# A linear attention, token mixing and gated MLP chain: the list order of all its steps replaced by a written-out order

## The chip, the cores and the metric

The kernel runs on one core of a Trainium2 chip. The core has five engines with an instruction queue each: TensorE (PE in the profile, with its weight loads as PEld), VectorE (DVE), ScalarE (ACT), GpSimd (POOL) and SyncE (SP). Each works off its queue in order and waits at semaphores for the others. DMAs are issued here from SP's and POOL's queues. The metric is the device time of one execution in microseconds; less is better. What is given of a kernel is the median of its runs.

## The reference

```python
def _attn_ref(q, k, v, alpha):              # 4 batches, 8 heads, 768 positions, 48 wide
    for t in range(S):
        state = alpha[:, :, t, :, None] * state + einsum('bhd,bhe->bhde', k[:, :, t], v[:, :, t])
        y[:, :, t] = einsum('bhd,bhde->bhe', q[:, :, t], state)
...
def _moe_ref(x, w_theta, w_tok_r, w_tok_i, w_ch):       # x is 4 x 768 x 384
    theta = x @ w_theta
    y = einsum('ts,bsd->btd', w_tok_r, x * cos(theta)) + einsum('ts,bsd->btd', w_tok_i, x * sin(theta))
    u = x + y
    return u + maximum(u @ w_ch, 0.0)
...
def _moe2_ref(x, w_in, w_spatial, b_spatial, w_out):
    h = maximum(x @ w_in, 0.0)                          # 1024 wide
    u, v = h[..., :512], h[..., 512:]
    v_n = (v - mean(v)) / sqrt(var(v) + 1e-06)
    v_s = einsum('ts,bsd->btd', w_spatial, v_n) + b_spatial[None, :, None]
    return (u * v_s) @ w_out
```

The three run one after the other, the output of each being the x of the next.

## The kernel before

The attention is cut into 24 units: 4 batches with 6 blocks of 128 positions each. A unit holds two chunks of 64 positions for all heads. Large products are made of three passes each: a float32 operand is split into a high part (a cast by ScalarE) and a low part (a subtraction by VectorE), and high by high, high by low and low by high are added up in PSUM.

**A unit's steps in the first stage.** SP loads alpha (`load_al`, tile `al`, two buffers), q and k (`load_qk`) and v (`load_v`). VectorE makes the running products of alpha with two scans and a reciprocal (`att_scan`, L515 to L519, tiles `al` and `heads`) and scales q and k with them (`att_qk`, L527). TensorE makes the scores (`att_a`, L541) and the transposed k (`att_k`, L565); VectorE masks the scores (`att_mask`, L549, tiles `ax` and `am`), one half of which a DMA moves to other partitions (`move_a`, `ay`). State update and output are small products on quarters of the array (`att_u` L582, `att_y` L624; from unit 6 on one step `att_uy` makes the output of a unit and the update of the next), and VectorE takes the state on in short steps (`att_s` L592 writes `ss`, `att_t` L605 writes `tmp`). The last reader of a unit's `al` is its second `att_s`, and with that the load of the unit two later may go. The output x is transposed (`tr_p` L652), split (`tr_h` on ScalarE, `tr_l` L674 on VectorE, tile `xh`) and multiplied by w_theta in two parts (`th_p`, L684 for the high part of x, L687 for the low part). Then theta's fraction is taken (`th_k` on ScalarE, `th_r` L701 on VectorE, tile `r`), cosine and sine are made on ScalarE, multiplied by x (`z_m` L720) and split (`z_h` L724, `z_l` L728, tile `zs`). Token mixing (`tokmix`, L751) multiplies these parts by the token weights, in three column blocks and a real and an imaginary part, and collects a batch's six units in five PSUM banks (tiles `acc`). One bank is set to zero beforehand (`acc_zero`, L760). When a batch is through, VectorE adds x (`evac`, L765), and the channel mixing follows (`ch_h`, `ch_l`, `ch_p` L793, `ch_e` L803).

**The weights.** They are handed in as 64-bit floats. POOL's queue loads 16 pieces (`raw`, two buffers), ScalarE and VectorE make float32 of them (`top` L412, `join` L418) and split them (`high` L430, `low` L438).

**The second stage.** Per batch: v products (`v_p` L930), their norm (`v_r`, `v_b`, `v_w` on POOL, `v_n`) and split, gate products (`g_u` L1003 with the relu `g_r` L1034), spatial mixing (`g_s` L1042 in batch 0; in batches 1 to 3 seven smaller products `g_p` L1071 in place of eight, whose left and right sides are mixed by VectorE), the gating (`g_b`, `g_c`, `g_m` L1108, split by `g_h` and `g_l`) and the output (`o_p` L1129, `o_e`, `o_d`).

**What sets the order.** The code doesn't issue at once: each step is entered in a table with its engine, its cost, the steps that it comes after and the tiles that it holds. `latest` gives every step a due time, counted back from its followers; to it come offsets by the kind of step (the table `OFF`, further ones for the first and last batch, for units and for weight pieces). `order` then goes through a model of the engines and takes, on each free engine, the ready step that is due first. The result is one list, and each engine's queue is that list's steps for it. The last lines are

```python
    with tc.manual_schedule():
        for key in order(latest(steps, due)):
            runs[key](*key[1:])
```

Of the kernel before, what the change touches and what calls it, by code (L numbers as in the profile page):

```python
# [42 lines left out]
T0 = 512  # L43
# [6 lines left out]
OFF = {  # L50
# [6 lines left out]
    "ce": -972.0, "cd": 3157.87, "raw": -151.03, "bits": -1303.6, "sgn": 1953.06, "mag": -330.42, "mul": 468.42,  # L57
    "high": -305.28, "low": 395.16, "v": 17.67, "vr": -218.91, "vb": -247.26, "vw": 2596.17, "vm": 1232.85,
    "vh": -1569.89, "vl": -130.09, "g_u": 11.48, "g_r": -360.31, "g_s": -2682.77, "g_m": -600.69, "g_h": -2547.65,
    "g_l": 1286.47, "o_p": 19.23, "o_e": 2160.27, "x2h": -2423.22, "x2l": 194.68, "x2": 255.08,  # L60
}
SLACK = 1.5
# [8 lines left out]
OFF0 = {  # L71
# [6 lines left out]
}  # L78
OFF3 = {
# [6 lines left out]
}  # L86
UNIT = {
    "0": -1233.88, "1": -299.19, "2": -157.26, "3": -128.17, "4": -124.98, "5": -85.26, "6": -419.5, "7": -274.72,
    "8": -235.21,
}  # L90
PIECE = {
    "0": -1201.98, "1": -1780.19, "2": -1381.94, "3": -878.12, "4": -78.08, "5": 154.16, "6": 764.79, "7": -371.9,
    "8": 64.23, "9": 826.07, "10": 983.66, "11": 1836.51, "12": 3937.87, "13": -2365.1, "14": 839.22, "15": 324.21,
}
# [14 lines left out]
PE_WINDOW = 4096 / 1200  # L109
PE_BUSY = {"att_a": 0.85, "att_u": 0.75, "att_y": 0.75, "att_uy": 0.75}  # L110
QUARTERS = ("att_a", "att_u", "att_y", "att_uy")
TO_QUARTERS = 0.09
TO_WHOLE = 0.12
TOGETHER = 10.0
FIRST = {"pe": 0.8, "dve": 1.6, "act": 2.2, "pool": 1.5, "dma": 0.74, "none": 0.0, "queue": 1.5}
ISSUE = {"dma": 0.44, "queue": 0.57}
AHEAD = {"dma": 0.9, "queue": 1.1}


def order(steps):  # L120

    keys = list(steps)
    at = {k: (round(steps[k][0], 3), n) for n, k in enumerate(keys)}
    follow = {k: [] for k in keys}  # L130
    left = {}
    users = {}
    for k, (_, _, _, _, after, tiles, _) in steps.items():
        left[k] = len(after)
        for p in after:
            follow[p].append(k)
        for x in tiles:
            users[x] = users.get(x, 0) + 1
    held_by = {}
    placed = set()  # L140
    ready = {e: [] for e in ("pe", "dve", "act", "pool", "dma", "none", "queue")}
    free = dict(FIRST)
    quarters = {k: k[0] in QUARTERS for k in keys}
    tiled = False
    port = 0.0
    lines = {"dma": [], "queue": []}
    clock, turn = 0.0, 0
    when = {}
    heap = []
    n = 0  # L150

    def push(t, what, k):
        nonlocal n
        heapq.heappush(heap, (t, n, what, k))
        n += 1

    def rates():
        on = [q for q in lines.values() if q]
        whole = sum(steps[q[0][0]][6] for q in on)
        return [(q, steps[q[0][0]][6] / whole) for q in on]  # L160

    def advance(now):
        nonlocal clock
        for q, r in rates():
            q[0][1] -= (now - clock) * r
        clock = now

    def plan(now):
        nonlocal turn
        turn += 1  # L170
        to = min((now + max(q[0][1], 0.0) / r for q, r in rates()), default=None)
        if to is not None:
            push(to, "moved", turn)

    def finish(k, t):
        push(t, "done", k)
        for f in follow[k]:
            left[f] -= 1
            when[f] = max(when.get(f, 0.0), t)
            if not left[f]:  # L180
                push(when[f], "ready", f)

    for e, t in free.items():
        push(t, "tick", None)
    for k in keys:
        if not left[k]:
            push(0.0, "ready", k)
    out = []
    cold, win, busy = True, 0, {}
    while heap:  # L190
        now = heap[0][0]
        while heap and heap[0][0] <= now + 1e-9:
            _, _, what, k = heapq.heappop(heap)
            if what == "ready":
                heapq.heappush(ready[steps[k][1]], (at[k], k))
            elif what == "done":
                for x in steps[k][5]:
                    users[x] -= 1
                    if not users[x]:
                        held_by[x[0]] -= 1  # L200
            elif what == "sent":
                advance(now)
                lines[steps[k][1]].append([k, steps[k][6]])
                plan(now)
            elif what == "moved" and k == turn:
                advance(now)
                for q in lines.values():
                    if q and q[0][1] < 1e-7:
                        x, _ = q.pop(0)
                        finish(x, now + steps[x][3])  # L210
                plan(now)
        moved = True
        while moved:
            moved = False
            for e, q in ready.items():
                if free[e] > now + 1e-9:
                    continue
                held = []
                while q:
                    if e == "pe" and TOGETHER:  # L220
                        best = min(q, key=lambda x: (x[0][0] - TOGETHER * (quarters[x[1]] == tiled), x[0][1]))
                        q.remove(best)
                        heapq.heapify(q)
                        k = best[1]
                    else:
                        _, k = heapq.heappop(q)
                    _, _, cost, lag, _, tiles, shared = steps[k]
                    fresh = [x for x in tiles if x not in placed]
                    want = {}
                    for x in fresh:  # L230
                        want[x[0]] = want.get(x[0], held_by.get(x[0], 0)) + 1
                    if any(want[x[0]] > x[1] for x in fresh):
                        held.append((at[k], k))
                        continue
                    for x in fresh:
                        held_by[x[0]] = held_by.get(x[0], 0) + 1
                        placed.add(x)
                    out.append(k)
                    moved = True
                    if e == "pe":  # L240
# [21 lines left out]
                    if e != "none":  # L262
                        free[e] = t
                        push(t, "tick", None)
# [1286 lines left out]
```

## Time and profile before

| | us |
|---|---|
| median of 3 runs (594.84 to 598.99) | 595.09 |
| span of the profiled execution, first to last instruction | 592.2 |
| TensorE busy | 561.6 |
| VectorE busy | 440.4 |
| ScalarE busy | 255.5 |
| GpSimd busy | 26.0 |

The profile is of one execution. The time of a run is taken around the whole execution, so it lies a little above a span; 2.9 us lie between this span and the median. Busy times are unions over the span, and a matmul's end is modelled, so a row of TensorE can hold a short delay. In the rows, "PE" is TensorE, "DVE" VectorE, "ACT" ScalarE, and SPq an issue from SyncE's queue; L-numbers are lines of the kernel before.

### The profile page before, as it was taken

What the parts mean: (1) busy time and instruction counts of PE and PEld (TensorE: products, weight loads), DVE (VectorE), ACT (ScalarE), POOL (GpSimd) and SP (SyncE); (2) the same over time, 40 slices, a digit from 0 to 9 for tenths busy, and PEclk for the clock granted to TensorE, in tenths of its full rate; (3) what the DMA queues carried; (4) which work ended last, traced back from release to release, by engine and by line L of the source; (5) the groups of instructions that cost most, each with busy time, mean ns of one, the idle gap of its engine ahead of it and who ended that gap; (6) DMA issues with size and microseconds to landing.
All of it is one profiled execution on the core that took longest, in us unless ns stands there. A gap on an engine that the chain in (4) does not pass through costs nothing.

```text
span 592.2 us, 13513 instructions
## 1 busy us (share of the span) xinstructions
PE 561.6 (95%) x5749; PEld 511.1 (86%) x5749; DVE 440.4 (74%) x770; ACT 255.5 (43%) x475; POOL 26.0 (4%) x45
## 2 busy tenths in 40 slices
PE   1579999999999999999999999999999999999997
PEld 1467878888888898888998899999999899998997
DVE  5999999989787875889355798958636586658650
ACT  2566656435344523544444444434324441435222
POOL 1101100000000000000000001000000010001000
PEclk9999999999999999999999999999999999999999
DMA  7866757435424225333016564001002100210002
GB/s 278 300 219 225 245 185 261 137 99 178 140 93 144 81 69 172 119 99 94 10 52 217 190 226 145 0 1 54 27 2 81 66 14 0 81 68 13 1 1 80
DMA packets 29500, 66.15 MB, mean 112 GB/s; under 512 B 3072, under 2 KB 14336, under 8 KB 29184
## 3 DMA queue, kind: packets, MB, share of 16 engines
q1 hardware_dynamic: 27264, 53.49, 26.8%
q0 software_dynamic: 2176, 11.80, 5.7%
q8 instruction: 45, 0.74, 0.5%
q14 instruction: 15, 0.12, 0.1%
HBM read 52.69 MB, written 9.44 MB: 105 GB/s over the span
## 4 chain that ended last, share of the span: by engine, by line
PE 65%; DVE 16%; DMA 8%; ACT 5%; issue 4%; POOL 1%; SPq 0%; DVEq 0%; POOLq 0%; ACTq 0%
PE acc L751 18%; PE acc L1071 11%; PE pu L1003 7%; PE psc L793 6%; PE po L1129 5%; PE psv L930 5%; PE sp L1042 3%; PE th L684 2%; DMA al<-in_al 2%; PE psuy L624 2%; DVE al L515 2%; DVE qk L527 2%; DMA raw<-in_w_ti 2%; DMA qk<-in_qk 1%; DVE vns L968 1%
## 5 line engine op out<-in xcount | busy, mean ns | idle before, releaser
L751 PE MATMUL acc<-w,zs 128*128 128x512 f32 (+1 forms) x864 | 171.2, 343 | 0.2 <-DVE acc L760 0.2
L751 PEld LDWEIGHTS acc<-w,zs 128*128 128x128 f32 x864 | 133.7, 188 | 17.2 <-DVE acc L760 0.5
L1003 PE MATMUL pu<-xs,w 128*128 128x384 f32 x288 | 53.1, 337 | 1.0 <-ACT ur L1034 0.6
L930 PE MATMUL psv<-w,xs 128*128 128x512 f32 x216 | 53.1, 394 | 0.0
L1129 PE MATMUL po<-w,gs 128*128 128x384 f32 x288 | 52.4, 337 | 0.0
L1003 PEld LDWEIGHTS pu<-xs,w 128*128 128x128 f32 x288 | 50.1, 188 | 2.4 <-ACT v L941 1.0
L1129 PEld LDWEIGHTS po<-w,gs 128*128 128x128 f32 x288 | 50.7, 188 | 0.7
L930 PEld LDWEIGHTS psv<-w,xs 128*128 128x128 f32 x216 | 40.3, 187 | 8.4
L793 PE MATMUL psc<-us,wch 128*128 128x384 f32 (+1 forms) x243 | 41.2, 320 | 0.3 <-DVE xT L803 0.3
L793 PEld LDWEIGHTS psc<-us,wch 128*128 128x128 f32 x243 | 38.0, 189 | 1.3 <-DVE xT L803 0.6
L1115 ACT CAST gs<-t 128x384 fp32r<-128x384 f32 x32 | 16.4, 512 | 50.8 <-DVE t L1108 50.8
L515 DVE TENSOR_TENSOR_SCAN al<-al,heads 112x536 f32<-112x536 f32 x24 | 30.5, 1269 | 7.5 <-DMA al<-in_al 7.5
L953 POOL TENSOR_TENSOR rs<-rs,mhalf 128x1 f32<-128x1 f32 x24 | 15.9, 664 | 441.8 <-DVE rs L950 441.8
L684 PE MATMUL th<-wth,xh 128*128 128x384 f32 x144 | 31.2, 352 | 3.4 <-ACT kt L569 1.0
L724 ACT CAST zs<-z 128x768 fp32r<-128x768 f32 x24 | 20.0, 833 | 27.0 <-PE acc L751 18.8
L728 DVE TENSOR_TENSOR zs<-z,zs 128x768 fp32r<-128x768 f32 x24 | 22.9, 954 | 11.8 <-ACT zs L724 11.5
L519 DVE TENSOR_TENSOR_SCAN al<-al,heads 112x536 f32<-112x536 f32 x24 | 30.6, 1275 | 0.8
L412 ACT ACTIVATE zeros<-raw 128x768 f16<-128x768 bf16 (+1 forms) x22 | 22.8, 1035 | 19.5 <-DMA raw<-in_w_ti 8.3
L684 PEld LDWEIGHTS th<-wth,xh 128*128 128x128 f32 x144 | 25.2, 194 | 6.1 <-ACT xT L661 3.0
L1071 PE MATMUL acc<-wt,vns 128*128 128x384 f32 x162 | 30.4, 338 | 0.0
L1071 PE MATMUL acc<-w,mx 128*128 128x384 f32 x162 | 30.4, 337 | 0.0
L527 DVE TENSOR_TENSOR qk<-qk,al 112x1024 f32<-112x1024 f32 x24 | 29.2, 1219 | 0.1
(122 smaller groups left out, 969.6 us busy)
## 6 DMA issues: line engine op xcount, KB each, us to landing
qk<-in_qk SPq DMA_DIRECT2D x24, 512.0 KB, 4.7
vd<-in_v SPq DMA_DIRECT2D x24, 288.0 KB, 3.9
al<-in_al SPq DMA_DIRECT2D x24, 268.0 KB, 3.7
raw<-in_w_ti POOLq DMA_DIRECT2D x6, 768.0 KB, 5.6
raw<-in_w_tr POOLq DMA_DIRECT2D x6, 768.0 KB, 5.0
out<-o SPq DMA_DIRECT2D x24, 192.0 KB, 1.8
x2d<-xT SPq DMA_DIRECT2D x6, 576.0 KB, 3.3
ay<-ax SPq DMA_DIRECT2D x48, 64.0 KB, 2.3
```

The lines of the kernel that those rows point to most:

```text
L412: nc.scalar.activation(out, c["top"].rearrange("p (c k) -> p c k", k=4)[:, :, 0], AF.Identity, scale=0.5)
L515: nc.vector.tensor_tensor_scan(out=back[:, ::-1], data0=line[:, ::-1], data1=one[:, ::-1], initial=1.0, op0=ALU.mult, op1=ALU.add)
L519: nc.vector.tensor_tensor_scan(out=line, data0=line, data1=one, initial=0.0, op0=ALU.mult, op1=ALU.add)
L527: nc.vector.tensor_tensor(out=x, in0=x, in1=st[u]["ar"], op=ALU.mult)
L684: nc.tensor.matmul(th, xh[:, 0, k], wth[:, pr, k], start=(k == 0 and pr == 0), stop=False)
L728: nc.vector.tensor_tensor(out=zs[:, 1], in0=st[u]["z"], in1=zs[:, 0].bitcast(F32), op=ALU.subtract)
L751: nc.tensor.matmul(acc[b, n][:, c0:c1], zs[:, pl, ri, m * 128:(m + 1) * 128], w[:, pr, t0:t1], start=first and n != 1, stop=last, skip_gro ...
L793: nc.tensor.matmul(ps, wch[:, pl, k, m * 128:(m + 1) * 128], us[:, pr, k], start=(n == 0), stop=(n == 3 * KD - 1),)
L930: nc.tensor.matmul(ps, xs2[:, pl, k, o:o + 128], win[pr, "v"][:, k], start=(n == 0), stop=(n == 3 * KD - 1),)
L1003: nc.tensor.matmul(pu, win[f // 2][:, pl, k * 256 + f % 2 * 128:k * 256 + f % 2 * 128 + 128], xq[b, h][:, pr, k], start=(n == 0), stop=(n ...
L1071: nc.tensor.matmul(g, left(b, n, j, pl, c), right(n, j, pr), start=(n in (1, 5, 6) and i == 0), stop=(i == 3 * NJ - 1), skip_group_check=n ...
L1129: nc.tensor.matmul(po, gs[b][:, pl, f, s * 128:(s + 1) * 128], wo[f // 2][:, pr, f % 2 * DM:(f % 2 + 1) * DM], start=(n == 0), stop=(n == ...
```

## The change

The model, its cost figures and all tables of offsets go. In their place stands `ORDER`, a list of 1709 numbers: the place of each step in the table in which the code enters them. The steps are issued in just that order. What a step issues is unchanged, and so are all tiles and their numbers of buffers. In two entries (`t_h` and `t_l`) a tile is added to those that the step holds; with the model gone, nothing reads that any more.

```diff
-import heapq
...
-OFF = {
-    "al": 696.51, "qk": 555.29, "vt": 1126.11, "sc": -158.32, "kh": -256.6, "q": 2901.57, "A": -999.99, "m": -63.76,
...
-def order(steps):
...
-def latest(steps, due):
...
+ORDER = [int(n) for n in """
+129 130 66 166 131 6 0 167 132 133 67 68 169 69 11 7 168 138 205 134 139 70 140 8 136 1 9 141 170 142 175 12 178 135 165 137 171 176 10 204 13 177 173
...
-            return step(OFF[name] + more.get(name, 0.0) + UNIT.get(str(u), 0.0), eng, cost, fn, u, *args, after=after, tiles=tiles, by=by)
+            return step(0.0, eng, cost, fn, u, *args, after=after, tiles=tiles, by=by)
...
     with tc.manual_schedule():
-        for key in order(latest(steps, due)):
+        keys = list(steps)
+        for key in (keys[n] for n in ORDER):
             runs[key](*key[1:])
```

Of TensorE's 452 steps some 190 keep their place among each other (a longest common sequence), of VectorE's 614 some 310, of ScalarE's 449 some 240, of SP's 152 some 100. The 16 loads on POOL's queue stand as before. No step moves by more than 44 places on its engine. Lines are those of each kernel: the new one is 174 lines shorter above the steps.

The first place is VectorE after the low part of a w_theta piece, where unit 2 is scaled. In the rows, `qk` is the scaling of q and k, `al` with `heads` the scans, `xh` the low part of x, `wf` the joined and `w` the split weight, `ss` a state step, `r` theta's fraction, `ax` and `am` the two masks. Before:

```order
L527 TENSOR_TENSOR qk<-qk,al 112x1024
L592 TENSOR_TENSOR ss<-tmp,al 112x192
L515 SCALAR_TENSOR_TENSOR al<-al,heads 112x536
L518 RECIPROCAL al<-al 112x8
L519 SCALAR_TENSOR_TENSOR al<-al,heads 112x536
L674 TENSOR_TENSOR xh<-pst,xh 128x384
L418 SCALAR_TENSOR_TENSOR wf<-raw,zeros 128x768
L549 TENSOR_TENSOR ax<-acc_383,cst_sb 128x256
L527 TENSOR_TENSOR qk<-qk,al 112x1024
L549 TENSOR_TENSOR am<-acc_384,cst_sb 128x256
L438 SCALAR_TENSOR_TENSOR w<-wf,w 128x768
L674 TENSOR_TENSOR xh<-pst,xh 128x384
```

The same place in the new order:

```order
L353 TENSOR_TENSOR qk<-qk,al 112x1024
L500 TENSOR_TENSOR xh<-pst,xh 128x384
L245 SCALAR_TENSOR_TENSOR wf<-raw,zeros 128x768
L341 SCALAR_TENSOR_TENSOR al<-al,heads 112x536
L344 RECIPROCAL al<-al 112x8
L345 SCALAR_TENSOR_TENSOR al<-al,heads 112x536
L265 SCALAR_TENSOR_TENSOR w<-wf,w 128x768
L418 TENSOR_TENSOR ss<-tmp,al 112x192
L245 SCALAR_TENSOR_TENSOR wf<-raw,zeros 128x768
L527 SCALAR_TENSOR_TENSOR r<-kk,th 128x384
L353 TENSOR_TENSOR qk<-qk,al 112x1024
```

The split of unit 0's x and a weight's join went ahead of unit 3's scan; a split weight, a second join and unit 0's theta went ahead of the scaling of unit 3, and its split of unit 1's x is further down than these rows.

The second place is TensorE when it comes to unit 3: `psk` is the transposed k, `th` the theta products of unit 1, `psa` the scores, `psy` the attention output of unit 2, `acc` with `zs` token mixing. Before:

```order
L565 MATMUL psk<-cst_sb,qk 128x112 x4
L684 MATMUL th<-wth,xh 128x384 x6
L541 MATMUL psa<-qk 64x64 x16
L687 MATMUL th<-wth,xh 128x384 x3
L624 MATMUL psy<-ss,qk 64x48 x4
L624 MATMUL psy<-vd,ay 64x48 x4
```

The same place in the new order:

```order
L391 MATMUL psk<-cst_sb,qk 128x112 x4
L510 MATMUL th<-wth,xh 128x384 x6
L513 MATMUL th<-wth,xh 128x384 x3
L367 MATMUL psa<-qk 64x64 x16
L577 MATMUL acc_513<-w,zs 128x512
L577 MATMUL acc_514<-w,zs 128x256
```

The second theta part went ahead of the scores, and token mixing of unit 0 went ahead of the attention output of unit 2.

The third place is VectorE between the last reading of unit 4's alpha (`ss`, which frees the buffer for unit 6) and the scan of unit 6. `tmp` and `ss` are state steps, `z` and `zs` the product with x and its split. Before:

```order
L592 TENSOR_TENSOR ss<-tmp,al 112x192
L549 TENSOR_TENSOR ax<-psa,cst_sb 128x256
L605 TENSOR_TENSOR tmp<-psu,ss 112x192
L549 TENSOR_TENSOR am<-psa,cst_sb 128x256
L592 TENSOR_TENSOR ss<-tmp,al 112x192
L720 TENSOR_TENSOR z<-z,x 128x768
L418 SCALAR_TENSOR_TENSOR wf<-raw,zeros 128x768
L605 TENSOR_TENSOR tmp<-psu,ss 112x192
L728 TENSOR_TENSOR zs<-z,zs 128x768
L592 TENSOR_TENSOR ss<-tmp,al 112x192
L515 SCALAR_TENSOR_TENSOR al<-al,heads 112x536
```

The same stretch in the new order:

```order
L418 TENSOR_TENSOR ss<-tmp,al 112x192
L245 SCALAR_TENSOR_TENSOR wf<-raw,zeros 128x768
L431 TENSOR_TENSOR tmp<-psu,ss 112x192
L527 SCALAR_TENSOR_TENSOR r<-kk,th 128x384
L554 TENSOR_TENSOR zs<-z,zs 128x768
L265 SCALAR_TENSOR_TENSOR w<-wf,w 128x768
L375 TENSOR_TENSOR ax<-psa,cst_sb 128x256
L418 TENSOR_TENSOR ss<-tmp,al 112x192
L431 TENSOR_TENSOR tmp<-psu,ss 112x192
L245 SCALAR_TENSOR_TENSOR wf<-raw,zeros 128x768
L418 TENSOR_TENSOR ss<-tmp,al 112x192
L341 SCALAR_TENSOR_TENSOR al<-al,heads 112x536
```

Two joins, a split weight and `r` stand in between now, and a `z` and a mask have gone elsewhere.

## Rows read from the trace of the kernel before

**Rows 1.** The page, part 1: busy us, share of the span, instructions.

```profile
PE 561.6 (95%) x5749; PEld 511.1 (86%) x5749; DVE 440.4 (74%) x770; ACT 255.5 (43%) x475; POOL 26.0 (4%) x45
```

**Rows 2.** Busy time by stretch: engines in order, then granted clock, DMA share, GB/s.

```profile
core 0: us, PE busy (x) PEld busy (x) DVE busy (x) ACT busy (x) POOL busy (x), PEclk, DMA share, GB/s
0.00:34.00 34.00, 14.64 (x293) 12.45 (x293) 26.09 (x43) 12.25 (x20) 4.50 (x11) 1.00 0.80 283
34.00:45.00 11.00, 8.56 (x196) 6.60 (x192) 10.97 (x20) 10.23 (x20) 1.06 (x2) 1.00 0.68 212
45.00:110.00 65.00, 62.52 (x896) 53.27 (x895) 62.56 (x93) 41.38 (x73) 4.48 (x8) 1.00 0.67 227
110.00:150.00 40.00, 39.73 (x586) 34.90 (x585) 34.65 (x59) 17.95 (x35) 0.00 (x0) 1.00 0.39 128
150.00:345.00 195.00, 193.44 (x2465) 171.58 (x2464) 143.60 (x230) 81.80 (x155) 1.64 (x2) 1.00 0.35 114
345.00:592.20 247.20, 242.76 (x1331) 232.28 (x1329) 162.53 (x328) 91.92 (x175) 14.30 (x22) 1.00 0.14 49
```

**Rows 3.** Timeline of VectorE in the opening: start, duration, line, tiles, idle before.

```profile
1.62 0.48 DVE L760 MEMSET acc<- 128x512 f32 x1
...
24.47 0.96 DVE L418 SCALAR_TENSOR_TENSOR wf<-raw,zeros 128x768 uint32<-128x768 uint32 x1 [0.85 <-ACT zeros L412]
...
28.93 1.22 DVE L527 TENSOR_TENSOR qk<-qk,al 112x1024 f32<-112x1024 f32 x1
30.06 0.35 DVE L592 TENSOR_TENSOR ss<-tmp,al 112x192 f32<-112x192 f32 x1
30.33 1.27 DVE L515 TENSOR_TENSOR_SCAN al<-al,heads 112x536 f32<-112x536 f32 x1
...
33.06 0.53 DVE L674 TENSOR_TENSOR xh<-pst,xh 128x384 fp32r<-128x384 f32 x1
33.51 0.95 DVE L418 SCALAR_TENSOR_TENSOR wf<-raw,zeros 128x768 uint32<-128x768 uint32 x1
```

**Rows 4.** Timeline of TensorE from 30 to 45 us, the same columns.

```profile
30.20 1.01 PE L565 MATMUL acc<-cst_sb,qk 112*128 112x112 f32 x4 [1.41 <-DVE qk L527]
30.89 2.27 PE L684 MATMUL th<-wth,xh 128*128 128x384 f32 x6
33.08 1.13 PE L541 MATMUL acc<-qk 48*64 48x64 f32 x32
...
37.59 1.33 PE L684 MATMUL th<-wth,xh 128*128 128x384 f32 x6 [1.00 <-ACT kt L569]
38.85 0.69 PE L541 MATMUL psa<-qk 48*64 48x64 f32 x32
...
43.09 0.55 PE L652 MATMUL pst<-cst_sb,x 128*128 128x128 f32 x3 [1.30 <-ACT x L640]
...
47.16 1.31 PE L684 MATMUL th<-wth,xh 128*128 128x384 f32 x6 [0.65 <-ACT xT L661]
```

**Rows 5.** Timeline of SyncE's queue near 67 us: issues.

```profile
67.18 0.33 SPq L500 DMA_DIRECT2D al<-in_al  x1
```

**Rows 6.** Timeline of VectorE from 66.5 to 73.2 us.

```profile
66.80 0.35 DVE L592 TENSOR_TENSOR ss<-tmp,al 112x192 f32<-112x192 f32 x1
67.07 0.42 DVE L549 TENSOR_TENSOR ax<-psa,cst_sb 128x256 f32<-128x256 f32 x1
67.40 0.35 DVE L605 TENSOR_TENSOR tmp<-psu,ss 112x192 f32<-112x192 f32 x1
...
68.26 0.95 DVE L720 TENSOR_TENSOR z<-z,x 128x768 f32<-128x768 f32 x1
69.13 0.95 DVE L418 SCALAR_TENSOR_TENSOR wf<-raw,zeros 128x768 uint32<-128x768 uint32 x1
...
71.13 0.35 DVE L592 TENSOR_TENSOR ss<-tmp,al 112x192 f32<-112x192 f32 x1
72.45 1.27 DVE L515 TENSOR_TENSOR_SCAN al<-al,heads 112x536 f32<-112x536 f32 x1 [0.97 <-DMA al<-in_al]
```

**Rows 7.** Waits of VectorE, 150 to 345 us: us in total, times, longest.

```profile
DVE al L515 <- DMA al<-in_al: 5.3, 6, 1.4
```

**Rows 8.** Waits of TensorE, 345 us to the end, the same columns.

```profile
PE pu L1003 <- ACT ur L1034: 0.6, 1, 0.6
```

More of the change, by code (lines that the diff above doesn't have):

```diff
@@ L108 @@
 SSB = 5
[L109 to L115, printed above, removed]
-ISSUE = {"dma": 0.44, "queue": 0.57}
-AHEAD = {"dma": 0.9, "queue": 1.1}
-def order(steps):
[L128 to L240, printed above, removed]
-                        if quarters[k] != tiled:
-                            cost += TO_WHOLE if tiled else TO_QUARTERS
-                            tiled = quarters[k]
-                        while now >= (win + 1) * PE_WINDOW:
-                            f = busy.get(win, 0.0) / PE_WINDOW
-                            cold = f < (0.86 if cold else 0.59)
-                            win += 1
-                        if cold:
-                            rest = (win + 1) * PE_WINDOW - now
-                            cost *= 2
-                            if cost > rest and busy.get(win, 0.0) + rest >= 0.86 * PE_WINDOW:
-                                cost = (cost + rest) / 2
-                        t, w = now, win
-                        while t < now + cost:
-                            to = min(now + cost, (w + 1) * PE_WINDOW)
-                            busy[w] = busy.get(w, 0.0) + (to - t) * PE_BUSY.get(k[0], 1.0)
-                            t, w = to, w + 1
-                    if shared and e not in lines:
-                        cost += max(now, port) - now
-                        port = now + cost
-                    t = now + cost
-                    if e != "none":
-                        free[e] = t
-                        push(t, "tick", None)
-                    if e in lines:
-                        push(t + AHEAD[e], "sent", k)
-                    else:
-                        finish(k, t + lag)
-                    if e != "none":
-                        break
-                for h in held:
-                    heapq.heappush(q, h)
-    if len(out) != len(steps):
-        raise RuntimeError("the steps wait for each other")
-    return out
@@ L278, in latest @@
-def latest(steps, due):
-    follow = {k: [] for k in steps}
-    left = {}
-    for k, v in steps.items():
-        for p in v[4]:
-            follow[p].append(k)
-    for k in steps:
-        left[k] = len(follow[k])
-    todo = [k for k in steps if not left[k]]
-    start = {}
-    while todo:
-        k = todo.pop()
-        _, eng, cost, lag, after, _, shared = steps[k]
-        t = min((start[f] for f in follow[k]), default=math.inf) - SLACK * (cost + lag + (shared if eng in ("dma", "queue") else 0.0))
-        start[k] = min(t, due.get(k, math.inf))
-        for p in after:
-            left[p] -= 1
-            if not left[p]:
-                todo.append(p)
-    return {k: (start[k] + v[0],) + v[1:] for k, v in steps.items()}
+ISSUE = {"dma": 0.44, "queue": 0.57}
@@ L301, in attention_mixer_kernel @@
+ORDER = [int(n) for n in """
[50 rows of a table added]
+""".split()]
 @with_exitstack
@@ L1278, in attention_mixer_kernel @@
         kev = [
-            step(OFF["ev"], "dve", 0.95, evac, b, m, after=[("tokmix", u, m, 1)] + [("tr_t", b * NS + i) for i in range(NS)], by=t + m,
+            step(0.0, "dve", 0.95, evac, b, m, after=[("tokmix", u, m, 1)] + [("tr_t", b * NS + i) for i in range(NS)], by=t + m,
                  tiles=[xt, *(ta[n] for n, *_ in acc_parts(m))])
@@ L1384, in plain @@
                 t += 3.12
-                k = step(OFF["g_m"], "dve", 0.48, g_b, b, f, h, after=[k, klb], tiles=[bank, ("t1", 2, (b, f, h)), ("f", FB, "t1")], by=t + 0.5)
+                k = step(0.0, "dve", 0.48, g_b, b, f, h, after=[k, klb], tiles=[bank, ("t1", 2, (b, f, h)), ("f", FB, "t1")], by=t + 0.5)
                 close(b, f, h, k)
@@ L1421, in out_of @@
             f = c + 2 * i
-            k = step(OFF["g_m"], "dve", 0.48, g_c, b, c, i, h, after=after, tiles=[bank(x), ("t1", 2, (b, f, h)), ("f", FB, "t1"), *more], by=t)
+            k = step(0.0, "dve", 0.48, g_c, b, c, i, h, after=after, tiles=[bank(x), ("t1", 2, (b, f, h)), ("f", FB, "t1"), *more], by=t)
             close(b, f, h, k)
@@ L1433, in seven @@
         k7 = product(7, [g2])
-        g3 = step(OFF["g_r"], "dve", 0.48, g_3, b, c, after=[k7, g2], tiles=[bank(1), sm, p1], by=t)
+        g3 = step(0.0, "dve", 0.48, g_3, b, c, after=[k7, g2], tiles=[bank(1), sm, p1], by=t)
         gate(b, c + 2, 0)
```

112 lines of the change are left out of this document (46 added, 66 removed), and 66 rows, old and new, of tables (OFF, OFF0, OFF3, ORDER).

## The prediction

> **What bounds the kernel now.** I read the busy shares first [rows 1]: TensorE (PE) is busy 95% of a span of 592.2 us. A share over the span mixes stages, so the next view is the table by stretch [rows 2]. PE idles 19.4 of the first 34.0 us (34.00 less 14.64), 2.4 from 34 to 45, 2.5 from 45 to 110, 0.3 to 150, 1.6 to 345 and 4.4 in the rest, of which 3.3 are the end behind its last matmul (output copy and store). No instruction is added or removed, so only idle time can go. Behind 34 us that is 2.44 + 2.48 + 0.27 + 1.56 + 1.1 = 7.9 us, to which come short delays inside rows that the profile calls busy.
>
> The second thing to see in [rows 2] is VectorE (DVE). From 34 to 45 it is busy 10.97 of 11.00 us, from 45 to 110 62.56 of 65.00. There it is the supplier: a unit's token mixing can't start before VectorE has split its z. The timeline [rows 3] shows that line without a gap, and PE standing behind it [rows 4]: 1.41 us for qk, 1.00 for a copy, 1.30 for x. So until about 110 us an order is judged by what VectorE does ahead of each PE step, and after that by short waits on a full PE.
>
> **The change part by part.**
>
> *The first 34 us: nothing.* The weight queue keeps its order word for word, and so do the first six loads. The zeroing of an accumulator (0.48 us, [rows 3]) leaves the free time ahead of the first scan and goes between two masks near 19 us. VectorE is then 0.4 us late, but it waits 0.85 us at 24.47 for a weight that is still being loaded, which hides it. Without that cover it would cost 0.4. Up to the scaling of unit 2's q and k at 28.93 both orders hold the same VectorE work.
>
> *34 to 45 us: a loss of 0.5.* Start-to-start costs from [rows 3] and [rows 6]: scan 2.73 with its reciprocal (30.33 to 33.06), qk 1.13, split of xh 0.45, weight join, weight low part and each z step 0.87, mask 0.33, small state step 0.27. After unit 2's qk (done at 30.06) the old line to unit 3's qk is ss, scan, xh, join, mask, qk: 0.27 + 2.73 + 0.45 + 0.87 + 0.33 + 1.13 = 5.8 us, so 35.8, as the trace has it. The new line is xh, join, scan, low, ss, join, r, qk: 0.45 + 0.87 + 2.73 + 0.87 + 0.27 + 0.87 + 0.45 + 1.13 = 7.6, so 37.7. PE comes there at about 35.9 and waits 1.9. Then the second half of unit 1's theta needs a split of xh that stands 3.6 us later than before (41.1), and PE, there at 39.3, waits another 1.9. That is 3.8 us of idle time for 2.4. On the other side the split of z of unit 0 stands 1.7 us earlier (two masks, two state steps and one r, 0.66 + 0.54 + 0.45, no longer stand ahead of it), and PE has its first token mixing at 42.7 in place of 44.17 [rows 4], with 2.0 us of attention work put behind it. 42.7 + 2.0 is 44.7, which is 0.5 behind 44.17. Bounds: 1.4 (the idle time alone) and -1.5 (the earlier start alone).
>
> *45 to 110 us: a gain of 1.9.* I set every PE step against the last VectorE step that it needs, with the same costs in both orders. The old order then leaves PE waits of 0.9, 0.9, 1.1, 0.3, 1.0, 0.1, 0.6, 0.1 and 0.5, together 5.6; the new 0.1, 0.7, 1.2, 0.9, 0.1, 0.5 and 0.1, together 3.6. So 2.0 less on paper. One more term is in no such sum: VectorE's own wait of 0.97 us at 72.45 for alpha of unit 6 [rows 6]. SP issues that load at 67.18 [rows 5], when the old buffer is read for the last time (ss at 66.80), and 4.4 us of VectorE work lie between that and the scan. In the new order it is 5.4 us (join, tmp, r, zs, low, ax, ss, tmp, join, ss), so the wait goes. Together -3.0. The trace, however, shows visible idle time of 2.48 in all here, which can't fall under nothing, and waits on ScalarE that the sum leaves out. I take 1.9, between 0 and 3.0, nearer to the row.
>
> *110 to 150 us: 0.2.* The PE work that stands between batch 0's last token mixing of the third column block and the reuse of its banks grows from two steps of 1.05 us to 6.0 us, which covers the two copies out (1.02 us for a pair). PE idles 0.27 there at all [rows 2]. Bounds 0 and 0.3.
>
> *150 to 345 us: 1.0.* VectorE waits six times for alpha here, 5.3 us together [rows 7]. The VectorE work between the freeing of the buffer and the scan changes for those six units from 2.9, 2.7, 2.5, 2.3, 1.1, 3.5 to 4.9, 2.5, 3.5, 4.1, 2.3, 5.5 us. That takes away about 3.8 of the 5.3. PE sees only part of it: it idles 1.56 us in this stretch, so the bounds are 0 and 1.6, and I take 1.0.
>
> *345 us to the end: 0.3.* The longest wait is 0.61 us at a gate product that waits for ScalarE's relu [rows 8]: its PSUM bank comes free after t_mix, g_b, a weight split and g_m. In the new order g_m comes ahead of the weight splits, which saves one step of 0.47. Against that, a gate product ahead of the plain gating must wait for a late eviction of the channel mixing, which I work out as 0.35 us. Bounds 0.4 more and 1.1 less. The last six output products and their stores are hardly touched: their 3.3 us stay.
>
> Sum: +0.5 - 1.9 - 0.2 - 1.0 - 0.3 = -2.9 us. The span of 592.2 becomes 589.3. Around the span of the profiled execution lie 2.9 us to the median of the runs shown (595.09), and these stay: **592.2 us**.
>
> TensorE's clock is one thing that moves with the waits. The theta product of six matmuls takes 2.27 us at 30.89 and 1.33 at 37.59 [rows 4]: in the opening PE runs at the lower of its two levels (1.2 GHz) though the view by stretch prints a granted clock of 1.00 there too, and it rises after PE has worked without a break from 30.2. The old gaps of 1.00, 1.30 and 0.65 us leave it high (the next theta runs at the short time). The new order has two gaps of 1.9 us close together, which no row of this trace shows. The Trainium skill, "TensorE: Matmul & The Clock Gate", section "HAM oscillation — how this bites in real kernels", says that waits between groups of matmuls can throttle the clock again, each time at the price of a slow stretch. By that rule the time would be up to that of the third rival.
>
> **The rivals.** (1) *No gain: the waits only change their place.* For it: the new order has more PE waits at 35 to 41 us, and VectorE's work ahead of 110 us is the same sum. Against it: the alpha loads get more lead in nearly every unit. All gains at 0 and the loss at 0.5 to 1.4 give 595.6 to 596.5.
>
> (2) *All waits go.* For it: the gaps between linked PE steps grow nearly everywhere behind 110 us (banks reused, state to state). Then all 7.9 us of idle time behind 34 us fall away but for the 3.8 that VectorE forces, and the short delays inside busy rows with them (some 4): 595.1 - 8 = 587. Against it: VectorE's line.
>
> (3) *Slower: the clock falls in the two gaps at 36 to 41 us.* PE then does its work at half speed from there for N us and loses N/2. The later waits of 0.7, 1.2 and 0.9 us take up 2.8 of it. With N = 6 it costs 0.2, so hardly shows. It decides once N passes 11.4: then 5.7 - 2.8 = 2.9 eats the forecast gain. With N = 19, until 60 us, 9.5 - 2.8 = 6.7 is lost: 592.2 + 6.7 = 599. For it: in the first 34 us PE works in bursts between waits and never rises before a stretch without a break. Against it: behind 41 us the new order gives PE token mixing without a wait up to 56.
>
> (4) *VectorE waits more for alpha.* Unit 2's load now stands behind a move of the scores whose mask is 2.7 us later (issue 20.5 for 17.81, scan at 25.34, [rows 3, 5]), and for units 4, 8 and 9 the lead shrinks by 0.8, 0.3 and 0.9 us. With 5.3 us from issue to scan as at 72.45 that is 0.5 + 0.5 + 2.1 + 1.2 = 4.3, and the sum becomes 596.5. Against it: unit 8 had a lead of 3.4 and did not wait.
>
> **How the numbers follow.** The forecast, with its own range of 588 to 595, gets 0.60; rivals 1 and 4 together 0.16; rival 2 0.16; rival 3 0.08. The bounds of the terms reach from +1.8 to -7.5, so 587.6 to 596.9. The range that holds 8 in 10 leaves out the far ends of rivals 2 and 3: 587.0 to 597.0. One per cent is 6 us, about what a measurement of this kernel tells from no change: under 589.1 lie rival 2 and the low end of the forecast, 0.20; over 601.0 rival 3 at its worst and what I don't see, 0.08; between them 0.72.
>
> **What would show it.** In the profile after: PE idle in the first 34 us within 1 us of 19.4; about 3.8 us idle from 34 to 45, with waits for qk and xh; no wait of VectorE for alpha near 70 us and under 2 us of them from 150 to 345; the last 3.3 us unchanged. If theta products at 42 to 55 us take over 2 us, rival 3 is at work. The prediction is wrong if the new order changes the first 34 us, which I hold to be fixed by the weight loads, or if ScalarE, which I left out, is late at the z chain.

## The result, and the profile after

The new order is faster: 588.05 us median of 4 runs (585.51 to 591.64) against 594.97 for the kernel before (593.66 to 598.99), a ratio of 0.9878 with a 95% interval of 0.9834 to 0.9922. On a second chip, with 8 and 25 runs, it was 589.12 against 593.42, 0.9931 (0.9893 to 0.9969). The forecast of 592.2, 2.9 under before, has the sign right; its 2.9 us are 0.42 of the 6.9 measured here and 0.67 of the 4.3 on the second chip.

The profiled execution was the slowest of the four: span 589.9 us, 2.3 under that of before. The view by stretch of the kernel after, columns as in [rows 2], with the last stretch ending at its span:

```profile
0.00:34.00 34.00, 15.76 (x267) 13.46 (x267) 27.21 (x44) 13.11 (x21) 5.03 (x12) 1.00 0.83 292
34.00:45.00 11.00, 8.10 (x114) 6.70 (x115) 9.91 (x19) 8.35 (x15) 1.06 (x2) 0.63 0.51 157
45.00:110.00 65.00, 64.25 (x988) 55.16 (x987) 61.88 (x94) 40.61 (x74) 3.94 (x7) 0.98 0.65 211
110.00:150.00 40.00, 40.00 (x593) 35.66 (x592) 35.90 (x62) 19.46 (x38) 0.00 (x0) 1.00 0.50 159
150.00:345.00 195.00, 194.39 (x2475) 172.62 (x2474) 146.33 (x236) 85.16 (x159) 1.74 (x3) 1.00 0.37 119
345.00:589.90 244.90, 240.99 (x1319) 230.97 (x1318) 159.01 (x321) 88.33 (x171) 12.81 (x21) 1.00 0.13 46
```

Two things stand against [rows 2]. PE's idle time is smaller in every stretch but the second: 18.24 for 19.36, 2.90 for 2.44, 0.75 for 2.48, 0.00 for 0.27, 0.61 for 1.56 and 3.91 for 4.44 us. And in the second stretch the granted clock is 0.63, where it was 1.00. Cut finer, the same view shows when:

```profile
34.00:36.00 2.00, 0.98 (x64) 0.99 (x64) 1.39 (x4) 2.00 (x5) 0.13 (x1) 1.00 0.55 225
36.00:38.00 2.00, 0.56 (x12) 0.42 (x5) 2.00 (x4) 1.97 (x5) 0.41 (x1) 0.73 0.48 84
38.00:40.00 2.00, 2.00 (x9) 2.00 (x8) 2.00 (x4) 1.46 (x3) 0.00 (x0) 0.50 0.89 345
...
46.00:48.00 2.00, 2.00 (x49) 1.53 (x50) 1.93 (x3) 0.12 (x1) 0.00 (x0) 0.71 0.92 362
48.00:50.00 2.00, 2.00 (x45) 1.77 (x38) 1.10 (x2) 1.45 (x4) 0.00 (x0) 1.00 0.30 51
```

The clock falls at about 37 us and is back at about 47. The timeline of TensorE after shows what it did before the fall, and what the lower level does to the rows:

```profile
35.02 0.61 PE L408 MATMUL acc<-vd,kt 64*64 64x48 f32 x30 [1.34 <-ACT kt L395]
...
37.61 1.00 PE L391 MATMUL psk<-cst_sb,qk 112*128 112x112 f32 x4 [1.44 <-DVE qk L353]
38.29 2.27 PE L510 MATMUL th<-wth,xh 128*128 128x384 f32 x6
41.01 1.33 PE L513 MATMUL th<-wth,xh 128*128 128x384 f32 x3 [0.45 <-DVE xh L500]
42.26 1.13 PE L367 MATMUL psa<-qk 48*64 48x64 f32 x32
43.33 4.09 PE L577 MATMUL acc<-w,zs 128*128 128x512 f32 x12
```

Two waits of 1.34 and 1.44 us, then a theta product of 2.27 us where [rows 4] has 1.33 at 37.59, and twelve token mixing products in 4.09 us. The Trainium skill, "TensorE: Matmul & The Clock Gate", section "HAM oscillation — how this bites in real kernels", tells of a clock that falls again in the waits between groups of matmuls, there longer waits for DMA; this trace agrees that it falls, but here in the second of two waits that are both under 1.5 us.

The first of the two waits is not one that the forecast names. ScalarE's timeline after:

```profile
33.53 1.06 ACT L239 ACTIVATE zeros<-raw 128x768 f16<-128x768 bf16 x1 [2.21 <-DMA raw<-in_w_ti]
34.46 0.51 ACT L395 COPY kt<-acc 128x448 f32<-128x448 f32 x1
```

Unit 2's transposed k (`kt`) is copied behind a weight step that waits 2.21 us for its load; in the old order `kt` stands ahead of that weight. VectorE's timeline has the scaling of unit 2 at 27.89, 1.04 us earlier than in [rows 3], and its waits for alpha from 45 to 345 us, 6.3 us in the kernel before with the one of [rows 6], are all but gone:

```profile
DVE al L341 <- DMA al<-in_al: 0.2, 1, 0.2
```

### The profile page after: what moved, and what is told of

Its sections match the earlier page's. It is cut to its first block, busy times and chain, and to the rows that moved or that the text cites. A ratio compares the mean times of both kernels' runs of the same rounds, so it can differ in the third digit from the quotient of the medians.

```text
span 589.9 us, 13476 instructions
## 1 busy us (share of the span) xinstructions
PE 563.5 (96%) x5749; PEld 514.6 (87%) x5749; DVE 440.2 (75%) x770; ACT 255.0 (43%) x475; POOL 24.6 (4%) x45
## 4 chain that ended last, share of the span: by engine, by line
PE 84%; DVE 5%; DMA 3%; ACT 2%; issue 2%; POOL 0%; DVEq 0%; ACTq 0%; POOLq 0%; SPq 0%
PE acc L577 24%; PE acc L897 11%; PE pu L829 9%; PE po L955 8%; PE psv L756 6%; PE psc L619 6%; PE sp L868 4%; PE th L510 4%; PE psuy L450 3%; PE psa L367 2%; PE th L513 2%; PE psuy L408 2%; DMA raw<-in_w_ti 2%; PE psk L391 1%; PE pst L478 1%
## 5 line engine op out<-in xcount | busy, mean ns | idle before, releaser
L577 PE MATMUL acc<-w,zs 128*128 128x512 f32 (+1 forms) x864 | 173.2, 346 | 0.0
L779 POOL TENSOR_TENSOR rs<-rs,mhalf 128x1 f32<-128x1 f32 x24 | 14.5, 609 | 441.9 <-PE psv L756 249.8
L897 PEld LDWEIGHTS acc<-w,mx 128*128 128x128 f32 x162 | 28.7, 188 | 0.0
L897 PEld LDWEIGHTS acc<-wt,vns 128*128 128x128 f32 x162 | 28.6, 188 | 0.1
```

Source lines behind the costliest of these rows:

```text
L577: nc.tensor.matmul(acc[b, n][:, c0:c1], zs[:, pl, ri, m * 128:(m + 1) * 128], w[:, pr, t0:t1], start=first and n != 1, stop=last, skip_gro ...
L897: nc.tensor.matmul(g, left(b, n, j, pl, c), right(n, j, pr), start=(n in (1, 5, 6) and i == 0), stop=(i == 3 * NJ - 1), skip_group_check=n ...
```

## The experiments

All were run five rounds beside the kernel before, in three groups on three chips; before had 593.93, 593.42 and 593.59 us there. The edits are edits of the order alone (moved steps, or a list put together from the two), except where products are added; lines are those of the new kernel (two higher in experiment 8). Theory A was at first: the spread of the new kernel and half its possible gain are TensorE's clock in the opening. Theory B, its rival: the clock's fall is hidden behind VectorE, and times differ by the arrival of loads.

To compare traces I use **TensorE's lag**: the time at which it starts a step, less the best durations (from these traces) of all steps ahead of it. The lag grows when TensorE waits or runs slow, and is given at marks of work done, of 538 us in all. Differences to the trace of before (us; minus is further ahead; the number of an experiment in brackets):

```
work done            15     25     35     60     70    110    160    200    298    537
time in before       46     58     69     97    107    150    204    245    345    588
new order          +2.6   +1.3   +2.5   +0.5   +0.7   -0.1   -2.1   -1.7   -1.3   -2.3
new, again (5)     -1.5   -2.9   -1.6   -3.6   -3.4   -4.2   -6.2   -5.8   -6.8   -7.8
kt first (1)       -1.0   -2.2   -1.0   -3.1   -2.9   -3.6   -5.6   -5.3   -6.5   -7.3
kt, qk first (2)   +2.0   +0.8   +1.9   -0.2   +0.1   -0.7   -2.1   -1.8   -3.0   -3.8
filled (8)         -0.9   -2.0   -0.9   -3.0   -2.7   -2.9   -4.2   -3.9   -5.1   -5.8
before to 48 (6)   +1.4   +1.1   +3.1   +1.0   +1.2   +0.5   -1.5   -1.2   -2.4   -3.1
before to 96 (10)  +0.1   +0.1   +2.2   +1.8   +1.7   +0.9   -1.1   -0.7   -0.3   -1.3
after to 48 (7)    +0.5   +1.1   +0.8   +0.2   +0.2   +0.2   -0.4   -0.4   -0.3   -0.3
after to 96 (9)    -1.7   -3.1   -1.8   -3.8   -2.0   -1.8   -3.1   -3.1   -3.3   -3.3
two steps (12)     -2.3   -2.3    0.0   +0.1   +0.1   +0.1   -0.9   -0.9    0.0   -0.1
```

Each row is one profiled execution. That of experiment 5 is the fastest of its eight runs, that of the new order the slowest of its four, so their ends lie on either side of the medians. Behind the mark at 107 us the rows sort by the order that stands there: the seven with the new order gain 3.0 to 4.4 us on the kernel before from that mark to the end, the three with the old order 0.2 to 1.3.

**1. ScalarE: kt ahead of the weight** (the new order's rows on ScalarE, one moved).

```diff
 L257 ACTIVATE w<-wf 128x768
-L239 ACTIVATE zeros<-raw 128x768
 L395 COPY kt<-acc_360 128x448
+L239 ACTIVATE zeros<-raw 128x768
```

> The changed kernel, with one step moved on ScalarE: the copy of unit 2's transposed k (kt) ahead of the weight step (top) that stood ahead of it and waited 2.21 us for its load. Theory A (the spread of the changed kernel, 585.5 to 591.6 us, is TensorE's clock, which falls in two waits near 34 and 37 us and comes back about 10 us later): the first of the two waits goes, the second grows to some 2.4 us, since VectorE's qk still comes at 37.5; granted clock still under 1.000 in some runs, median 586 to 590. Theory B (the spread is the timing of DMAs all along, and the clock's fall costs nothing, since VectorE is late there anyway): median 588 as the changed kernel, with the same spread.

589.65 us (586.70 to 590.74), ratio 0.9932 (0.9908 to 0.9957): as the new order itself on a second chip (0.9931). In its profile the first wait is gone and the second has grown to 1.94 us, of the some 2.4 that A said; no run has a granted clock of 1.000 (0.993 to 0.997). The median does not tell A from B. The five runs at 0.997 took 586.7 to 589.7 us, the three at 0.993 and 0.994 took 590.2 to 590.7.

**2. The same, and VectorE's scaling of unit 3 moved ahead.**

```diff
-L245 SCALAR_TENSOR_TENSOR wf<-raw,zeros 128x768
-L527 SCALAR_TENSOR_TENSOR r<-kk,th 128x384
 L353 TENSOR_TENSOR qk<-qk,al 112x1024
+L245 SCALAR_TENSOR_TENSOR wf<-raw,zeros 128x768
+L527 SCALAR_TENSOR_TENSOR r<-kk,th 128x384
```

> As the run before, and on VectorE unit 3's scaling of q and k ahead of a weight's join and unit 0's theta, so that neither of the two waits near 34 and 37 us is left. Theory A: no gap of over 1 us on TensorE from 34 to 42 us, granted clock 1.000 in every run, times within 2 us of each other around 585.5. Theory B: 588 with a spread of 3 us or more, as the changed kernel.

590.84 us (588.67 to 592.58), ratio 0.9942. The expectations of A miss: the gap does not go but moves, the clock is 0.991 to 0.997, and the times spread by 3.9 us. The median is nearer to B's 588, but 2.8 over it. TensorE's timeline of this kernel:

```profile
35.05 0.60 PE L391 MATMUL psk<-cst_sb,qk 112*128 112x112 f32 x4 [0.82 <-DVE qk L353]
36.38 2.29 PE L510 MATMUL th<-wth,xh 128*128 128x384 f32 x6 [0.73 <-DVE r L527]
40.33 1.33 PE L513 MATMUL th<-wth,xh 128*128 128x384 f32 x3 [1.66 <-DVE xh L500]
```

The second theta part starts at 40.33 although `qk` came early, since VectorE's split of x comes then.

**3 and 4. Halves, cut at 48 us.** The list is the first 150 steps of one order, then what is left in the other's.

```diff
+ORDER = before[:150] + [n for n in after if n not in before[:150]]   # 3; 4 with the two exchanged
```

> The first 150 steps (to about 48 us) in the order of before, the rest in the new order. Of the profiled executions the new order is behind by 0.5 us at 48 us with a fallen clock, and 2.8 us ahead of that at the end. Theory A: clock 1.000, and the gain behind 48 us alone: 3 us, so about 592. If the whole gain of the fast runs (8 us) lies behind the opening: 587.

> The first 150 steps in the new order, the rest in that of before. Theory A: clock under 1.000 in some runs; where it holds 1.000 the new opening is worth 8 less 3, 5 us, so about 590; where it falls, 595 or more. If all gain lies behind the opening: 595 to 598 in every run.

597.67 and 601.46 us, both slower than either kernel. The cut broke SyncE's queue: a load of q and k whose buffer was still in use stood ahead of unit 5's alpha, and VectorE waited for it 6.0 us in one and 7.1 in the other (waits of VectorE, kernel of 3):

```profile
DVE al L341 <- DMA al<-in_al: 6.0, 1, 6.0
```

So the medians of these two say nothing on the halves, but on what one load in the wrong place of that queue costs.

**5. The new order again**, unchanged, on the chip of 6 to 8.

> The changed kernel as it is, beside the kernel before on one chip. Theory A (its spread is TensorE's clock in the opening): runs with granted clock near 1.000 lie at 585 to 587, runs at 0.991 at 590 to 592, median about 588, ratio 0.988. Theory B: no order between clock and time.

589.12 us (586.15 to 594.10). Clock and time of its runs: 1.000 with 587.0, 588.1 and 590.5; 0.997 with 586.2 and 594.1; 0.994 with 588.3 and 589.9; 0.993 with 591.9. The order in that is loose, nearer to B. But the four runs of the result are in A's order without an exception (1.000 with 585.5, 0.997 and 0.994 with 588.0 and 588.1, 0.991 with 591.6), and so, by groups, are those of experiment 1; whether the low clock makes those runs slow or late loads make both is not shown. This time the profile is of the fastest run, 586.15 us, with a span of 584.4. By stretch, and on TensorE:

```profile
0.00:34.00 34.00, 15.96 (x308) 13.86 (x312) 27.76 (x45) 15.16 (x25) 5.03 (x12) 1.00 0.82 287
34.00:45.00 11.00, 8.94 (x160) 7.37 (x153) 10.93 (x20) 8.55 (x17) 1.06 (x2) 0.84 0.66 209
45.00:110.00 65.00, 64.24 (x968) 55.41 (x967) 63.24 (x100) 40.75 (x73) 3.94 (x7) 1.00 0.63 213
```

```profile
36.19 1.01 PE L391 MATMUL psk<-cst_sb,qk 112*128 112x112 f32 x4 [1.62 <-DVE qk L353]
36.87 2.27 PE L510 MATMUL th<-wth,xh 128*128 128x384 f32 x6
39.59 0.80 PE L513 MATMUL th<-wth,xh 128*128 128x384 f32 x3 [0.44 <-DVE xh L500]
40.31 0.69 PE L367 MATMUL psa<-qk 48*64 48x64 f32 x32
40.94 2.37 PE L577 MATMUL acc<-w,zs 128*128 128x512 f32 x12
```

Here the clock is low for 3 us only, and the slow theta product at 36.87 costs nothing, since the next step waits 0.44 us for VectorE up to 39.59 anyhow. Token mixing starts at 40.94. In the trace of before it is this row:

```profile
44.17 2.00 PE L751 MATMUL acc<-w,zs 128*128 128x512 f32 x10
```

**6 and 7. The halves again, with SyncE's queue mended** (one load each behind the alpha load).

```diff
 ORDER = before[:150] + ...       # 6
-load_qk 5 ahead of load_al 5
+load_qk 5 behind load_al 5
 ORDER = after[:150] + ...        # 7
-load_qk 6 ahead of load_v 4, load_al 5 and load_v 5
+load_qk 6 behind them
```

> The first 150 steps (to about 48 us) in the order of before, the rest in the new order, now with the load of unit 5's alpha ahead of its q and k, so that SyncE's queue does not block at the cut (that cost 6.0 us of waiting in the earlier attempt). The stall at the cut goes and 597.7 becomes about 591.5. If the gain of the change lies behind the opening (lag of TensorE behind its work: 3.6 us from work unit 40 to the end): 590 to 591, 3 us under before. If it lies in the opening: as before, 594.

> The first 150 steps in the new order, the rest in that of before, now with the load of unit 6's q and k behind v of unit 5, so that the queue does not block at the cut (7.1 us in the earlier attempt). If the gain lies behind the opening: 594 or a little over, as before. If the opening holds half of it: 591.

591.42 us (0.9974, 0.9946 to 1.0003) for 6, and 593.42 (0.9986, 0.9963 to 1.0010) for 7. Both lie nearer to what was expected if the gain lies behind the opening. The parts, -2.0 and 0.0, are less than the -4.3 of the whole, but the whole's interval (0.9893 to 0.9969) takes them in. The trace of 7 can't say what becomes of a lead, for it has none at 46 us: it waits 2.10 us for `qk` and 1.73 for xh, and its clock is 0.57 from 42 to 46 us.

**8. The two waits of TensorE filled with products of zeros.** They add zero to a bank that token mixing adds to later.

```diff
+FILL = {("tr_p", 1): 5, ("att_a", 2): 6}
...
             runs[key](*key[1:])
+            for _ in range(FILL.get(key, 0)):
+                nc.tensor.matmul(acc[0, 1][0:64, 0:128], heads[:, 0, 1:65], ident[:112, :],
+                                 start=False, stop=True, skip_group_check=True)
```

> The changed kernel with eleven small products of zeros added on TensorE, five in its wait near 34 us and six in that near 37 us, which add nothing to the bank that they go to. Theory A: TensorE's clock stays at its upper level through both waits, granted clock 0.998 or more in most runs, median 585 to 586. Theory B: 588 as the changed kernel, or up to 1 us more for the added work.

588.04 us (587.32 to 589.42), 0.9902 (0.9870 to 0.9935). TensorE's clock stays up, as A expected: 1.000 in four runs of six, and the theta product takes 1.31 us. But the time is not 585 to 586. Its spread is 2.1 us, where the new order had 6.1 and 8.0: that fits the first half of A, with six runs. TensorE's timeline of this kernel says why:

```profile
35.75 1.52 PE L1330 MATMUL acc<-cst_sb,heads 112*64 112x128 f32 x12
37.20 0.60 PE L393 MATMUL psk<-cst_sb,qk 112*128 112x112 f32 x4
37.57 1.31 PE L512 MATMUL th<-wth,xh 128*128 128x384 f32 x6
40.24 0.79 PE L515 MATMUL th<-wth,xh 128*128 128x384 f32 x3 [1.35 <-DVE xh L502]
```

What the faster clock gains at 37.57 is waited away at 40.24. So A falls as to the price: the median gains 1.1 us by holding the clock, which these runs don't tell from none. The length of the fall goes with the lag: the two profiles with some 10 us at the lower level, the new order's and that of 2, stand at +2.6 and +2.0 at 46 us; 1, 5 and 9, with 3 us, at -1.0 to -1.7, and 8, without a fall, at -0.9. So a short fall cost nothing here, and a long one goes with 3 to 4 us; that the clock alone makes these is not shown.

**9 and 10. Halves, cut at 96 us**, where both orders have issued the same loads and differ in 12 steps.

```diff
+ORDER = after[:332] + [n for n in before if n not in after[:332]]    # 9; 10 with the two exchanged
```

> The first 332 steps (to about 96 us) in the new order, the rest in that of before; at this cut both orders have issued the same loads and differ in 12 steps only, so no queue blocks at the seam. Of the profiled executions TensorE is 3.4 to 3.6 us further with its work at this point in the new order (when its clock does not fall for long) and gains 4.2 us more behind it. If the two parts add up: 590.0, and TensorE's lag at work unit 70 lies 3 us under that of before and stays there. If the lead is lost again behind the cut, as it was in the run cut at 48 us: 593.

> The other half: the first 332 steps in the order of before, the rest in the new one. If the parts add up: 593.4 less 4.2, so 589.2. If the gain behind the cut needs the lead that the new opening brings: 592 to 593.

593.20 us for 9 (1.0003, 0.9980 to 1.0026) and 591.25 for 10 (0.9958, 0.9944 to 0.9973). In the trace of 9 the lead of 3.8 us is there at 97 us, and 1.8 of it go in the next 10 us (a wait of 1.2 us for VectorE's xh in its profile), a seam of the two lists; its profiled run, 590.89, was its fastest. So 9 came out as expected if the lead is lost again, and 10 between its two cases. 10 shows a gain of 3.0 us from 107 us to the end and a loss of 2.1 at 58 to 69 us, of which experiment 12 tells more. In medians the new order behind the cut is worth 2.0 and 2.3 us (6 and 10), ahead of it 0.0 and 0.4 (7 and 9); of these only 10's is clear of the noise, and either pair's sum lies in the interval of the whole.

**11. Alpha waits put back into the new order.**

```diff
-att_scan 6, 13, 14, 15, 16, 17, 18 where the new order has them
+each 2 to 6 places further ahead on VectorE, about 2.2 us behind the issue of its load
```

> The changed kernel, with the scans of units 6 and 13 to 18 moved ahead on VectorE by two to six steps, so that each stands about 2.2 us behind the issue of its alpha load, as close as the kernel before has them. VectorE then waits for alpha about 1 us in each of them, 6 to 8 us together (0.3 now). If the price of an alpha wait is what the prediction took (0.9 for unit 6, 0.26 of a us for each us waited behind 110 us): 1.5 to 2.5 us slower than the changed kernel, 591 where that has 589. If TensorE's slack covers them: under 0.7 slower.

614.86 us (611.83 to 620.38): 21 slower than the kernel before on its chip and 26 slower than the new order on another, ten times the 2.5 us that were expected at most. VectorE waits for alpha 7.6 us from 45 to 345 us, as planned; TensorE waits in the same trace from 110 us on:

```profile
PE psuy L408 <- DVE ax L375: 3.0, 1, 3.0
PE psa L367 <- DVE xT L629: 2.7, 1, 2.7
PE acc L577 <- DVE acc L586: 2.6, 1, 2.6
PE psc L619 <- DVE xT L629: 2.0, 1, 2.0
PE acc L577 <- ACT zs L550: 2.0, 1, 2.0
```

None of them waits for a scan. They wait for what the scan was moved past (a mask, the zeroing of a bank, two sums of the channel mixing, and, through ScalarE, a product z), which now stands behind a wait and 2.7 us of scan; and from 150 to 200 us the granted clock is 0.84. Besides, the opening of this profile was late before any moved step came (unit 2's scaling at 30.59 us, 27.24 in experiment 5). So what stands behind a scan on VectorE can cost far more than the scan's wait; the price of the wait alone stays open.

**12. Two steps of the opening moved in the kernel before.**

```diff
-load_qk 2, load_v 1
+load_v 1, load_qk 2
-att_mask 0 0, att_mask 0 1, join 1
+join 1, att_mask 0 0, att_mask 0 1
```

> The kernel before, with two steps moved in its opening, as the new order has them: the load of unit 1's v ahead of unit 2's q and k, and a weight's join on VectorE ahead of the two masks of unit 0, so that the fourth weight load can be issued earlier. If the new opening's lead comes from the weight loads: unit 2's scaling at 28.0 instead of 28.9, the wait of 0.85 us for the weight at 24.5 gone, and 1 us faster, 592.4. If VectorE's line takes it up (the prediction's claim that the first 34 us give nothing): no change, 593.4.

593.18 us (0.9988, 0.9974 to 1.0002): no change that can be told. But the profile shows the lead that was expected, and more: unit 2's scaling at 26.66 (28.93 before), the wait of 0.85 us gone, TensorE 2.3 us ahead until 60 us. There it is lost to the last tenth, at one place. SyncE's queue and VectorE in this kernel:

```profile
53.14 0.33 SPq L331 DMA_DIRECT2D qk<-in_qk  x1
...
60.98 1.23 DVE L353 TENSOR_TENSOR qk<-qk,al 112x1024 f32<-112x1024 f32 x1 [2.23 <-DMA qk<-in_qk]
```

and the same two in the kernel before, with an earlier one of its queue:

```profile
23.80 0.38 SPq L505 DMA_DIRECT2D qk<-in_qk  x1
...
55.44 0.33 SPq L505 DMA_DIRECT2D qk<-in_qk  x1
...
60.98 1.23 DVE L527 TENSOR_TENSOR qk<-qk,al 112x1024 f32<-112x1024 f32 x1
```

This is unit 5's q and k. In the trace of both, the load lands at 60.89, and VectorE starts 0.09 us later; in the kernel before without a wait that a view shows. The load comes so late because the load at 23.80 is that of unit 6: it took one of the three buffers 50 us ahead of its use, and unit 5 had to wait until unit 3's was read. Experiments 6 and 10, which hold that old order of loads too, have the same place: there the load of unit 5's q and k, issued at 55.56 in 10, lands at 63.11, and VectorE stands still for 2.03 us ahead of the row below, which is the loss of 2.1 us in 10 (1.23 us and 63.25 in 6).

```profile
63.20 1.23 DVE L353 TENSOR_TENSOR qk<-qk,al 112x1024 f32<-112x1024 f32 x1 [2.03 <-DMA qk<-in_qk]
```

In the new order unit 6's load stands behind unit 5's, which is issued at 48.44 and lands at 51.86 in the first profile (44.33 and 49.60 in the second).

## Why the prediction was right and wrong

*The first 34 us: "nothing".* Wrong. The claim rested on the weight queue and the first six loads being the same. The seventh and eighth are not: v of unit 1 is issued ahead of unit 2's q and k, and the first weight lands at 9.1 us in the mean of the ten traces with that order (8.36 to 9.62), at 10.0 in that of the four with the old (9.45 to 10.45). And a join ahead of two masks frees a weight buffer earlier. VectorE has done 27.2 and 27.8 us of work by 34 us, for 26.1 before, and TensorE's lag is 1.2 and 1.5 us less there; its idle time is 18.24 and 18.04, where the prediction allowed 1 us around 19.4. Experiment 12 shows that these two steps alone make such a lead, and its trace shows where it goes: at unit 5's q and k, held back by the early load of unit 6's, which I had not followed on SyncE's queue at all. That moving this load too would keep the lead was not tried.

*34 to 45 us: "+0.5".* In the first profile the pieces came nearly as worked out: TensorE reaches unit 3's k at 37.61 (37.7 said), the split of x lets it go at 41.01 (41.1). Token mixing starts at 43.33 with the low clock (42.7 said, where 44.17 less the 1.7 of the text is 42.5), and the lag is +2.6 at 46 us. In that of experiment 5 VectorE's pieces come some 1.5 us earlier (36.19 and 39.59), token mixing starts at 40.94, and the lag is -1.5. TensorE idles 2.90 and 2.06 us, for 3.8 said. With the other profiles that hold the new opening (1, 2, 7, 8, 9) the lag at 46 us runs from -1.7 to +2.6. So the +0.5 up to there lies within what one order gives from run to run: the sum is near, and its two parts, a lead of some 1.5 us and a loss of up to 3.8, were not seen.

*45 to 110 us: "-1.9".* Right in the sum. TensorE's idle time falls from 2.48 to 0.75, the wait for alpha of unit 6 is gone, and the lag gains 1.9 between 46 and 107 us in both profiles of the new order.

*110 us to the end: "-0.2 - 1.0 - 0.3".* Right in idle time (0.27, 0.95 and 0.53 less in the first profile), and the last 3.3 us stay as said, but too small in all: the lag gains 0.8, 1.2 and 1.0 in the first profile and 0.8, 2.6 and 1.0 in that of experiment 5. In all seven traces with the new order there it gains 3.0 to 4.4, for 1.5 said. What is missing lay as short delays in rows that count as busy: TensorE's busy time falls from 561.6 to 559.6 us in experiment 5 with the same products and 3 us of low clock. For these the sum had no term; rival 2 named them. Which rows they are in is not shown. That the alpha waits on VectorE go is right (under 2 us said, 0.2 measured). That they are what TensorE gains by is not shown: experiment 11 could not part the wait from the steps behind it.

*The clock, rival 3.* It falls, for 10 us in one profile and 3 in the other, but ahead of the second of the two waits that were said: in the first profile in that for `qk`, behind one for `kt` that the forecast does not name, in the other in that for `qk`. The price is not half of that time in both: the 3 us cost nothing, because VectorE is the later one at 40 us either way, and what the 10 us cost is not parted from the rest.

So the profiled execution fits the forecast (-2.3 for -2.9) by two errors against each other: by 46 us it is 2.1 worse than said, behind 107 us 1.5 better. That is luck. The medians lie 4.3 and 6.9 under before, and of the new kernel's other 11 runs all have a higher mean clock than the profiled one's 0.991. The 588.05 of the result lies inside the range of 587.0 to 597.0, but nearer to rival 2's 587 than to 592.2, in the part under 589.1 that got a chance of 0.20; the 4.3 of the second chip would make 590.8 of 595.09, nearer to the forecast. The mechanism, idle time that goes as loads and VectorE come earlier, was right behind 45 us; the mis-sized term is the stretch behind 107 us, 1.5 said and 3.0 to 4.4 measured, and the opening, held for fixed, is the part that moves from run to run.

Of the kernels run, that of experiment 8 has the lowest ratio on its chip, 0.9902 for 0.9931, with intervals that overlap; none beats the new order beyond doubt.

## What to carry to other kernels

When an order changes, follow every queue, the loads' too, to the first place where the two lists hold different sets: a buffer taken early by a load for later is as good as a wait, though it shows none as long as engine and load arrive together. A lead is worth what the next fixed arrival lets through, so a part tried alone may show no gain at all, as in experiment 12. On an engine that is nearly always busy, idle time is only a part of what an order can give: here nearly half of the gain behind 107 us lay in short delays inside busy rows. Ask of a slow stretch what the engine would meet at its end before pricing it, and take more than one profile before a stretch of a few us is called better or worse.

## What was not expected of the hardware

A load issued 2.3 us earlier (53.14 for 55.44) landed at the same 60.89 us in experiment 12, after 7.75 us in place of 5.45; issued at 55.56 in experiment 10 it landed at 63.11, after 7.55. Weight loads were under way beside it in all three. TensorE's clock fell in the second of two waits of 1.34 and 1.44 us in one execution and stayed down for some 10 us; in another of the same kernel it fell in one of 1.62 and was up again after 3. In experiment 7 it didn't fall in a wait of 2.10 us (the theta product behind it, at 37.13, takes 1.30) but only at 42.0, behind a further one of 1.73. The view by stretch prints 1.00 for the first 34 us of the kernel before and of the new one, while the theta product at 30.89 and 29.85 takes 2.27 us, the lower level's time. The kernel before has runs with a mean granted clock of 0.991 and runs with 1.000 at the same times (593.4 and 592.9, for example), so that number alone does not rank its runs; but on two of the three chips its runs under 0.990, ten of 44, are the slowest, 595.0 to 598.1.
